# A new order for the opening of a fused layer norm, state-space scan and gated unit: roots by logarithm and exponential, four groups open, tiles turned in pairs

## The chip, the cores and the metric

The kernel runs on one core of one Trainium2 chip. Its time is device microseconds from the start to the end of one execution; runs of the kernel before gave 182.41, 182.43 and 182.47 us, median 182.43. A core has TensorE (PE: matrix products and transposes, which write to the eight banks of PSUM), VectorE (DVE), ScalarE (ACT: functions from loadable tables), GpSimd (POOL) and SyncE (SP, which here issues nearly all DMA transfers). Each engine takes its instructions strictly in its own order; they wait for each other by semaphores.

## The reference

The input is `x` of 2048 tokens by 448 features in bfloat16. Cut to what matters:

```python
xn = (x - mean(x)) / sqrt(var(x) + 1e-5)          # per token
# A: a diagonal complex scan over the tokens
Lam_bar = exp(exp(log_dt) * Lam)                  # 448 complex numbers
Bu = xn @ B_bar.T                                 # complex, 448 wide
h[t] = Lam_bar * h[t - 1] + Bu[t]
s = 2 * real(h @ C.T) + xn * Dskip
# B: a gated unit, 448 -> 1792 -> 448
d = (sigmoid(xn @ w_gate) * (xn @ w_up)) @ w_down
out = x + s * silu(d)
```

## The kernel before

The 2048 tokens are cut into four chunks of 512, a chunk into four blocks of 128 tokens. For a chunk, `xn` is made with tokens on the partitions and then turned, so that `xnT` has features on the partitions: four tiles `kt` of 128 rows that cover the 448 features. The 1792 columns of the gated unit are 14 groups `ft` of 128. A group needs two sums of 128 x 512 in PSUM, `g_ps` (gate) and `u_ps` (up), one bank each. 448 is three times 128 and 64 more, so a sum takes three products over 128 rows (`gu_wholes`) and one over 64 rows (`gu_halves`); the gate's 64 rows lie in partitions 0 to 63 of `wt` and the up's in 64 to 127, and the two run side by side in the two halves of the array. From the group `ft` 4 on, all products are cut into halves of 64 rows, the upper and the lower half run side by side (`beside_each`, line 507 in the profile), and a POOL instruction passes on that one half has ended before the other half adds to the same sum (a "word"). The state-space part makes `Bu` in units -1 to -4 (`bu_unit`), which stand among the groups; it turns `Bu` by a table of sines and cosines (`cosT`, `spm`) so that a real scan on VectorE does the complex one.

The order of the work is written by hand: `keep_order` ties every instruction to the one before it on its engine, in the order in which the Python code emits them. What this study is about is the opening, up to the first group that runs in halves (groups 4 and 5).

The steps of the opening, in the kernel before:

- DMA. ACT issues three short rows (`log_dt`, `Lambda_im`, `Lambda_re`, L141). SP issues the four token blocks of chunk 0 (one, one, and two in one transfer), the weights of groups 0 to 3 (`load_w(sync, 0, 512)`), those of groups 4 to 9, then the next chunk, and so on.
- TensorE. 31 products of an identity matrix with itself (`warm`, L195) whose result nobody reads; the three rows turned into columns (`turn_twice`, L200 to L202, into `tp_v`); the first two token blocks turned (`ln_turn`, four 128 x 128 transposes each, L282, into `tp_x`), a few warm products between; then groups 0 to 2 for the first 256 tokens, gates first, then ups; blocks 2 and 3 turned; and the rest of groups 0 to 3.
- Statistics. DVE takes mean and variance (`ln_stats`, L211 and L212) of blocks 0, 1 and 3; ACT takes those of block 2 (`ln_sum`, `ln_mean`, `ln_square`). The inverse root is a power of -0.5 on POOL (`ln_pow`, L241) behind an addition of epsilon. DVE normalises (`ln_norm`, L268) and copies the turned blocks from PSUM to `xnT` (`ln_out`, L285). `tp_x` is two tiles, one bank each; block 0 uses one and block 1 the other, and blocks 2 and 3 use them again.
- Constants. `emit_vecs` and `emit_angles` make the step angle and the decay; `emit_whole` (ACT, L417), `emit_frac` and `emit_abs` (DVE, L422 and L428) reduce the angles; `emit_sin` and `emit_cos` (ACT, L433 and L436) fill the second half of the tables, `emit_neg` (DVE, L445) negates, `emit_mirror` (POOL, L448 and L450) fills the first half by symmetry. The fractions and their absolute values have two buffers each.
- Evacuation. Groups 0 to 3 leave PSUM by a tanh on ACT (L713) and a copy on DVE (`up_copy`, L992). The sums of groups 4 and 5 are given the banks that the first of these free.
- ACT loads a table of functions three times: for the exponential (L923), for sine and tanh (L951), and for the sigmoid (L746).

The PSUM pool has eight buffers under one tag, so a ninth tile waits until the one whose place it takes has been read.

## Time and profile before

| | |
|---|---|
| median of three runs | 182.43 us |
| profiled execution, its own time | 182.76 us |
| its span, first to last instruction | 181.0 us |
| TensorE busy | 176.5 us, 98% |
| VectorE busy | 163.2 us, 90% |
| ScalarE busy | 114.2 us, 63% |
| GpSimd busy | 24.9 us, 14% |
| first product of groups 0 to 3 | 6.86 us |
| first product of groups 4 and 5 | 14.06 us |

How to read it: a timeline row has the start in us from the start of the span, the time it took, engine, source line, operation, tile written from tiles read, shapes, and how many were merged; a bracket names the idle time of the engine before it and what ended it. `128*128 128x256` is a product with 128 rows and 128 columns of weights over 256 moving columns. The time of a single product includes its way through the array (0.31 us for 128 columns before 6.6 us), so a row of several is read by the spacing of their starts. ACTq and SPq are rows of a sequencer that issues a transfer.

### The profile page before, as it was taken

The page shows a single profiled execution, that of the slowest core. Times are in us where ns is not written, and L with a number is a line of the kernel's source. Part 1 is how long each engine was busy: PE and PEld are TensorE (multiplying, and loading weights), DVE is VectorE, ACT ScalarE, POOL GpSimd, SP SyncE. Part 2 cuts the span into 40 slices and gives each one's busy share as a digit, 9 for nine tenths or more (in the row PEclk, how much of TensorE's full clock was granted, in tenths as well). Part 3 has the DMA queues.
Part 4 walks back from the last instruction along what each step waited for, and adds up shares of the span by engine and source line. Part 5 has one row for each costly group of instructions (what it writes and reads, how often), then busy time and mean ns, then how long its engine had stood idle before and what let it go on. Part 6 is the DMA issues. An engine that isn't in the chain of part 4 may idle for free.

```text
span 181.0 us, 4338 instructions
## 1 busy us (share of the span) xinstructions
PE 176.5 (98%) x1644; PEld 89.1 (49%) x1644; DVE 163.2 (90%) x332; ACT 114.2 (63%) x234; POOL 24.9 (14%) x59
## 2 busy tenths in 40 slices
PE   7999999999999999999999999999999999999993
PEld 7874444444544444544544444544554444545552
DVE  4799989999999869999999999599999999499993
ACT  3999678979577887988277767047137677144100
POOL 4786626513000000003000000000000000000000
PEclk9999999999999999999999999999999999999999
DMA  5899999993442104011610020020010100011012
GB/s 158 262 283 144 261 166 166 352 220 76 86 83 59 32 0 126 10 53 51 91 30 0 4 48 10 4 97 4 4 29 2 33 0 2 4 51 51 0 32 74
DMA packets 26347, 14.26 MB, mean 79 GB/s; under 512 B 16083, under 2 KB 26070, under 8 KB 26326
## 3 DMA queue, kind: packets, MB, share of 16 engines
q1 hardware_dynamic: 26320, 13.98, 34.5%
q8 instruction: 13, 0.21, 0.5%
q14 instruction: 8, 0.07, 0.1%
q10 hardware_dynamic: 6, 0.00, 0.0%
HBM read 7.69 MB, written 1.84 MB: 53 GB/s over the span
## 4 chain that ended last, share of the span: by engine, by line
PE 97%; DVE 1%; POOL 0%; issue 0%; POOLq 0%; DVEq 0%
PE g_ps L507 25%; PE u_ps L507 19%; PE d_ps L507 18%; PE bu L507 12%; PE y_ps L507 11%; PE d_ps L1106 6%; PE warm_ps L195 2%; PE g_ps L707 2%; PE u_ps L707 1%; PE tp_x L282 1%; PE g_ps L700 1%; DVE sg L854 0%; DVE o_l L860 0%; POOL ident L136 0%; POOL ident L135 0%
## 5 line engine op out<-in xcount | busy, mean ns | idle before, releaser
L507 PE MATMUL u_ps<-xnT,wu 64*128 64x512 bf16 x312 | 61.4, 376 | 0.0
L507 PE MATMUL g_ps<-xnT,wg 64*128 64x512 bf16 x312 | 53.4, 376 | 0.0
L746 ACT ACTIVATE sig<-g_ps 128x512 bf16<-128x512 f32 x52 | 29.2, 597 | 29.2 <-PE g_ps L507 28.6
L507 PE MATMUL bu<-xnT,bT 64*128 64x512 bf16 x168 | 37.4, 376 | 0.0
L507 PE MATMUL d_ps<-wd,hF 64*128 64x448 bf16 x336 | 32.3, 349 | 0.0
L507 PEld LDWEIGHTS <-wu 64*128 64x128 bf16 x312 | 22.4, 94 | 18.5
L746 ACT CAST ub<-u_ps 128x512 bf16<-128x512 f32 x52 | 29.3, 606 | 0.5 <-DVE hF L717 0.3
L507 PEld LDWEIGHTS <-wg 64*128 64x128 bf16 x312 | 18.9, 94 | 18.1 <-issue 0.2
L507 PEld LDWEIGHTS <-hF 64*128 64x128 bf16 x336 | 16.4, 94 | 15.6
L604 DVE TENSOR_TENSOR_SCAN wv<-r_col,st,ta 128x512 bf16<-128x512 f32 x18 | 22.7, 1276 | 0.2
L507 PE MATMUL y_ps<-ct,h 64*128 64x448 bf16 (+2 forms) x203 | 22.1, 343 | 0.0
L743 DVE TENSOR_TENSOR hF<-sig,ub 128x512 bf16<-128x512 bf16 x52 | 20.9, 413 | 0.4 <-ACT ub L746 0.3
L507 PEld LDWEIGHTS <-bT 64*128 64x128 bf16 x168 | 15.8, 94 | 10.0
L507 PE MATMUL g_ps<-xnT,wt 64*128 64x512 bf16 x52 | 19.6, 376 | 0.0
L507 PE MATMUL u_ps<-xnT,wt 64*128 64x512 bf16 x52 | 19.6, 376 | 0.0
L507 PEld LDWEIGHTS <-h 64*128 64x128 bf16 (+1 forms) x203 | 11.6, 95 | 9.9
L770 ACT ACTIVATE sigd<-d_ps 128x448 bf16<-128x448 f32 x12 | 6.6, 553 | 14.7 <-PE d_ps L507 14.7
L585 ACT CAST bus<-bu 128x512 bf16<-128x512 f32 x24 | 14.3, 597 | 2.2 <-PE bu L507 2.2
L241 POOL TENSOR_TENSOR rsd<-ve,mhalf 128x1 f32<-128x1 f32 (+2 forms) x8 | 6.9, 862 | 44.7 <-PE bu L507 43.9
L507 PEld LDWEIGHTS <-wt 64*128 64x128 bf16 x104 | 9.8, 94 | 6.2
L825 DVE TENSOR_TENSOR o_t<-y_ps,xn 128x448 bf16<-128x448 f32 x12 | 6.9, 618 | 4.8 <-PE y_ps L507 4.8
L1106 PE MATMUL d_ps<-wd,hF 128*128 128x448 bf16 x56 | 10.9, 353 | 0.0
(149 smaller groups left out, 238.5 us busy)
## 6 DMA issues: line engine op xcount, KB each, us to landing
wd<-in_B_w_down_dram SPq DMA_DIRECT2D x1, 1568.0 KB, 7.7
x<-in_A_x_dram SPq DMA_DIRECT2D x3, 448.0 KB, 6.4
out_dram<-o_t SPq DMA_DIRECT2D x6, 224.0 KB, 2.1
wg<-in_B_w_gate_dram SPq DMA_DIRECT2D x2, 256.0 KB, 3.1
wu<-in_B_w_up_dram SPq DMA_DIRECT2D x2, 256.0 KB, 3.6
bsw<-bus SPq DMA_DIRECT2D x4, 128.0 KB, 3.3
wsw<-wv SPq DMA_DIRECT2D x8, 64.0 KB, 1.9
c_re<-in_A_C_re_dram SPq DMA_DIRECT2D x1, 392.0 KB
```

The lines of the kernel that those rows point to most:

```text
L195: pe.matmul(warm_ps[:], lhsT=ident[:], rhs=ident[:], start=True, stop=True)
L241: pool.tensor_tensor(out=rsd[:, t:t + n, :], in0=ve[:, t:t + n, :], in1=mhalf[:, 0:n, :], op=ALU.pow)
L282: pe.transpose(tps[j % 2][:, kt, :], xb[:, j, K_ROWS[kt]:K_ROWS[kt] + P], ident[:])
L507: m = pe.matmul(self.t[:, n0:n1], lhsT=lhsT, rhs=rhs, start=self.done == 1, stop=self.done == self.n)
L585: empty = [lambda cc=cc: act.copy(out=bus[:, cc, :], in_=pst[cc][:]) for cc in range(2)]
L604: dve.tensor_tensor_scan(out=T["wv"][:, cc, :], data0=rb, data1=T["ta"][:, cc, :], initial=(0.0 if c == 0 else st[pt][:, cc, :]), op0=mul, ...
L707: pe.matmul(t[:, n0:n1], lhsT=wm[:, k, f0:f1], rhs=xnT[c][:, kt, n0:n1], start=(first and k == 0), stop=(not first and k == 2))
L743: dve.tensor_tensor(out=h[:], in0=sig[:], in1=ub[:], op=ALU.mult)
L746: u.empty = [lambda: act.activation(sig[:], gt[:], ACT.Sigmoid), lambda: act.copy(out=ub[:], in_=ut[:])]
L770: act.activation(sigd[:], ds[j][:], ACT.Sigmoid)
L825: dve.tensor_tensor(out=two_runs(o[:, i, :], HD, HD), in0=two_runs(ys[c, j + 2 * i][:], HD, HD), in1=xn_runs(c, j + 2 * i), op=ALU.add)
L1106: pe.matmul(ds[j][:], lhsT=hF[c, ft][:, j * P:(j + 1) * P], rhs=wd[:, ft, :], start=ft == 0, stop=ft == FT - 1)
```

## The change

It touches the opening only.

- The inverse roots of chunk 0 are made by ACT, as the exponential of -0.5 times the logarithm (`ln_inv`), and no longer by POOL. ACT's first table is one that holds both functions; it is loaded by an explicit instruction.
- The three rows are turned after 7 warm products, and 19 follow; ACT copies them out of PSUM, and the angles, steps and denominators follow at once on POOL.
- All eight sums of groups 0 to 3 are given their banks before the first product. `tp_x` is still two banks, but a bank holds two turned blocks: blocks 0 and 1 are turned into the first, blocks 2 and 3 into the second.
- All four groups' gates for the first 256 tokens come first, then the transposes of blocks 2 and 3, then all four ups, then all products over 64 rows (first and second 256 tokens), then the remaining products over 128 rows. So TensorE changes between 128-row and 64-row products three times.
- Fractions and absolute values come after the copies of blocks 2 and 3; the index products on ACT come after the fourth root.
- The mirrors go to groups 5 (two of them), 8 and 11; before, two were in the opening and two at group 5.
- For groups 4 to 9, the 64-row weights are loaded before the up weights.

```diff
-    def load_w(eng, f0, f1):
+    def load_w(eng, f0, f1, tails_first=False):
...
-        eng.dma_start(out=wu[:, 0:2, f0:f1], in_=rows(B_w_up, 0, 256))
-        eng.dma_start(out=wu[:, 2, f0:f1], in_=rows(B_w_up, 320, 448))
-        eng.dma_start(out=wt[0:64, f0:f1], in_=rows(B_w_gate, 128, 192))
-        eng.dma_start(out=wt[64:128, f0:f1], in_=rows(B_w_up, 256, 320))
+        up = ((wu[:, 0:2, f0:f1], rows(B_w_up, 0, 256)), (wu[:, 2, f0:f1], rows(B_w_up, 320, 448)))
+        tails = ((wt[0:64, f0:f1], rows(B_w_gate, 128, 192)), (wt[64:128, f0:f1], rows(B_w_up, 256, 320)))
+        for o, i in (tails + up if tails_first else up + tails):
+            eng.dma_start(out=o, in_=i)
...
-    load_w(sync, 512, 1280)
+    load_w(sync, 512, 1280, True)
...
-    def ln_pow_of(t, n, var, scale):
-        pool.tensor_scalar(out=ve[:, t:t + n, :], in0=var, scalar1=scale, scalar2=EPS, op0=ALU.mult, op1=ALU.add)
-        ln_pow(t, n)
+    lnv = w.tile([P, TPC, 1], FP32, name="lnv")
+
+    def ln_inv(t, var, scale=1.0):
+        act.activation(lnv[:, t, :], var, ACT.Ln, bias=epsb[:], scale=scale)
+        act.activation(rsd[:, t, :], lnv[:, t, :], ACT.Exp, scale=-0.5)
...
-            pe.transpose(tps[j % 2][:, kt, :], xb[:, j, K_ROWS[kt]:K_ROWS[kt] + P], ident[:])
+            pe.transpose(tps[j // 2][:, j % 2, kt, :], xb[:, j, K_ROWS[kt]:K_ROWS[kt] + P], ident[:])
 
     def ln_out(j):
-        dve.tensor_copy(out=xnT[0][:, :, j * P:(j + 1) * P], in_=tps[j % 2][:])
+        dve.tensor_copy(out=xnT[0][:, :, j * P:(j + 1) * P], in_=tps[j // 2][:, j % 2, :, :])
...
-        dve.tensor_copy(out=vec[:], in_=tp_v[:, :, 0:3])
+        act.copy(out=vec[:], in_=tp_v[:, :, 0:3])
...
-    act.activation(dummy[:], hpi[:], ACT.Exp)
-    warm(31)
-
-    ln_stats(0)
-    ln_pow_of(0, 1, mv[:, 0:1, 1:2], 1.0)
-    ln_stats(1)
-    ln_root(1, 1)
+    act.add_instruction(mybir.InstLoadActFuncSet(name=nc.get_next_instruction_name(), act_func_set_id=LN_AND_EXP,
+                                                 ins=[], outs=[]))
+    warm(7)
+    turn_twice(tp_v, rows, 3)
+    emit_vecs()
+    emit_angles()
+    emit_steps()
+    emit_den()
+    tps = [ps.tile([P, 2, KT, P], BF16, name="tp_x", tag="bank", bufs=8) for _ in range(2)]
+    gus = [(bank("g_ps"), bank("u_ps")) for _ in range(4)]
+    warm(19)
+
+    for j in range(2):
+        ln_stats(j)
+        ln_inv(j, mv[:, j, 1:2])
     ln_sum(2)
-    turn_twice(tp_v, rows, 3)
-    tps = [ps.tile([P, KT, P], BF16, name="tp_x", tag="bank", bufs=8) for _ in range(2)]
     ln_norm(0, 0)
     ln_turn(0, 0)
-    emit_vecs()
-    emit_angles()
-    warm(2)
+    ln_norm(0, 1)
+    ln_turn(0, 1)
+    warm(4)
+    ln_out(0)
+    ln_out(1)
     ln_mean(2, 1)
     ln_square(2)
-    ln_pow_of(2, 1, sums[:, 2:3, 1:2], 1.0 / D)
-    ln_norm(0, 1)
-    ln_turn(0, 1)
-    warm(5)
-    ln_out(0)
-    ln_out(1)
+    ln_inv(2, sums[:, 2, 1:2], 1.0 / D)
     ln_stats(3)
+    ln_inv(3, mv[:, 3, 1:2])
+    act.activation(K["r"][:], K["arg"][:], ACT.Exp)
     for pt in (0, 1, 3, 2):
         emit_whole(pt)
-    act.activation(K["r"][:], K["arg"][:], ACT.Exp)
-
     act.activation(dummy[:], hpi[:], ACT.Silu)
-    ln_pow_of(3, 1, mv[:, 3:4, 1:2], 1.0)
-
-    gus = [(bank("g_ps"), bank("u_ps")) for _ in range(3)]
-    for ft in range(3):
+
+    for ft in range(4):
         gu_wholes(0, ft, *gus[ft], True, 0, HC, (0,))
-    for ft in range(3):
-        gu_wholes(0, ft, *gus[ft], True, 0, HC, (1,))
-    ln_norm(0, 2)
-    ln_turn(0, 2)
-    emit_frac(0)
-    ln_norm(0, 3)
-    ln_turn(0, 3)
-    emit_abs(0)
+    for j in (2, 3):
+        ln_norm(0, j)
+        ln_turn(0, j)
     for j in (2, 3):
         ln_out(j)
-    emit_frac(1)
-    emit_abs(1)
-    emit_frac(3)
-    emit_abs(3)
-    emit_frac(2)
-    emit_abs(2)
-    for ft in range(3):
-        gu_halves(0, ft, *gus[ft], False, 0, HC)
-    gus.append((bank("g_ps"), bank("u_ps")))
-    gu_wholes(0, 3, *gus[3], True, 0, HC)
-    gu_halves(0, 3, *gus[3], False, 0, HC)
+    for pt in (0, 1, 3, 2):
+        emit_frac(pt)
+        emit_abs(pt)
     for ft in range(4):
-        gu_halves(0, ft, *gus[ft], True, HC, TC)
+        gu_wholes(0, ft, *gus[ft], True, 0, HC, (1,))
+    for n0 in (0, HC):
+        for ft in range(4):
+            gu_halves(0, ft, *gus[ft], n0 > 0, n0, n0 + HC)
     for ft in range(4):
         gu_wholes(0, ft, *gus[ft], False, HC, TC)
-    emit_steps()
-    emit_den()
...
-    for pt in (0, 1):
-        emit_mirror(pt)
-    for pt in (3, 2):
-        at(0, 5, 0.0, lambda pt=pt: emit_mirror(pt))
+    for pt, ft in ((0, 5), (1, 5), (2, 8), (3, 11)):
+        at(0, ft, 0.0, lambda pt=pt: emit_mirror(pt))
```

## The prediction

> **What bounds the kernel now.** I read the page's busy shares and its chain that ended last, then the timeline of TensorE (PE) until it no longer waits, then VectorE (DVE), ScalarE (ACT) and POOL beside it.
>
> ```profile
> PE 176.5 (98%) x1644; PEld 89.1 (49%) x1644; DVE 163.2 (90%) x332; ACT 114.2 (63%) x234; POOL 24.9 (14%) x59
> PE 97%; DVE 1%; POOL 0%; issue 0%; POOLq 0%; DVEq 0%
> ```
>
> TensorE is busy for 98% of the span and 97% of the last chain. In the windows view, 14.06 to 160.00 has TensorE busy for all 145.94 us. So the end stands at a fixed distance behind 14.06, where the steady groups (L507) begin: 181.0 - 14.06 = 166.9 us. The change is in front of that point, so the question is when the first L507 starts.
>
> ```profile
> 1.35 3.49 PE L195 MATMUL warm_ps<-ident 128*128 128x128 bf16 x31 [1.35 <-POOL ident L136]
> 4.77 0.23 PE L200 MATMUL tp_v<-ident,rows 3*128 3x3 bf16 x3
> 5.10 0.61 PE L282 MATMUL tp_x<-ident,xn 128*128 128x128 bf16 x4
> 5.74 0.61 PE L282 MATMUL tp_x<-ident,xn 128*128 128x128 bf16 x4
> 6.14 0.74 PE L195 MATMUL warm_ps<-ident 128*128 128x128 bf16 x5
> 6.86 1.14 PE L707 MATMUL g_ps<-xnT,wg 128*128 128x256 bf16 x9
> 8.82 0.73 PE L282 MATMUL tp_x<-ident,xn 128*128 128x128 bf16 x8
> 11.33 0.50 PE L707 MATMUL g_ps<-xnT,wg 128*128 128x256 bf16 x3
> 14.06 0.82 PE L507 MATMUL g_ps<-xnT,wg 64*128 64x512 bf16 x6
> ```
>
> Until 6.86 TensorE mostly does warm-up products (L195); from 6.86 to 14.06 it does real work without a hole. The spacing tells the clock: 31 warm products in 3.49 us are 0.107 us apart ((3.49 - 0.31) / 30), and so still at 6.14 to 6.57; from 6.86 on 256 columns take 0.109 each, half the price per column. The full clock came between 6.57 and 6.86. (The PEclk row shows 9 throughout and does not tell this.)
>
> What releases 6.86 is the normalisation of the first two token blocks:
>
> ```profile
> 4.14 0.18 DVE L212 BATCH_NORM_AGGREGATE mv<-stats 128x2 f32<-128x6 f32 x1
> 5.29 0.39 DVE L268 TENSOR_SCALAR xn<-x,mv,rsd 128x448 bf16<-128x448 bf16 x1
> 5.75 0.42 DVE L285 COPY xnT<-tp_x 128x512 bf16<-128x512 bf16 x1
> 6.39 0.42 DVE L285 COPY xnT<-tp_x 128x512 bf16<-128x512 bf16 x1 [0.21 <-PE tp_x L282]
> ```
>
> Second variance at 4.32, normalised block at 5.68, turned from 5.74, copied by 6.81, first product at 6.86. The first copy ran while the second block was still being normalised and turned.
>
> ScalarE and DVE release the PSUM banks that the first L507 group writes:
>
> ```profile
> 8.20 1.28 ACT L951 ACT_TABLE_LOAD   x1
> 9.60 0.40 ACT L433 ACTIVATE spm<-frac 128x256 bf16<-128x256 f32 x1
> 9.90 0.49 ACT L436 ACTIVATE cosT<-afrac,hpi 128x256 bf16<-128x256 f32 x1
> 12.02 1.17 ACT L713 ACTIVATE tanh<-g_ps 128x512 f32<-128x512 f32 x2
> ```
>
> The first tanh ends near 12.6, the first u copy (DVE L992, from 12.55) near 13.2: 0.9 us or more ahead of 14.06.
>
> **The change, part by part.**
>
> *Vectors first.* The row transposes move ahead of 19 warm products, behind 7. They need three row loads that ACT issues at 0.72, 1.27 and 1.51, as before; the trace's semaphore record has the last one landing at 3.10 (bounds: the x blocks' 2.0 us from issue to landing gives 3.5; the second row, 2.69). So TensorE does 7 warm products until 2.1, idles about 1 us, does the five row transposes from 3.14 (0.33, from 4.77 to 5.10 in the trace), then 19 x 0.107 = 2.03: until 5.50. The first token transposes stand behind them. That is the change's main price: with 31 warm products ahead, this queue was empty at 4.6.
>
> *Inverse roots.* POOL's two instructions (0.19 + 0.6, ready at 4.55 and 5.15) go; ACT gets a logarithm and an exponential for each block. No row shows a logarithm. Small activations take 0.18 to 0.21; a pointer as bias adds 0.09 (sine 0.40, cosine with hpi 0.49); so 0.28 + 0.04 + 0.19 = 0.51 a pair. Bounds: 0.42 without the pointer's share, and 1.0 if a logarithm cost as much as the 448-wide square (0.67, L228). ACT now does the vector copy (about 0.2, DVE's was 0.17) and dt first: 3.58 to 4.04. The first root is ready at 4.46, the second at 4.88 (behind its variance at 4.32). Normalised blocks at 4.89 and 5.31: earlier than before, but both before TensorE is free at 5.50. This gain is covered by the warm products; even the 1.0 bound moves the second block only to about 5.8, against the 5.93 at which its transposes start.
>
> *Pairs.* Both blocks are turned in 8 x 0.107: last start 6.25, end 6.56. They now share one bank and one tile, and the built order has the first copy wait for the last transpose of the second block. So the two copies stand one behind the other: 6.59 + 0.77 (two copies at 9.25 took that) = 7.36, and the first L707 at 7.4 instead of 6.86. One copy more on the path is worth 0.35 of that.
>
> *TensorE from there.* The same 48 products of 256 columns (5.23) and 8 pairs of 64-row products (8 x 0.11 = 0.88). A change of row mode costs 0.10: at 10.68 and 11.33 the step is 0.205 instead of 0.109. After: 12 gate products to 8.71; third block turned to 8.93; the fourth waits for its root. DVE: copies to 7.36, statistics and aggregate as from 6.73 (0.83) to 8.12; ACT 0.05 + 0.51 = 8.68; normalised at 9.1; turned from 9.15 to 9.43, a hole of 0.2. Then 12 up products to 10.74 (the copies that free the last bank end at about 10.3), change, 8 pairs, change, 24 products, change: 10.74 + 0.10 + 0.88 + 0.10 + 2.62 + 0.10 = 14.54. That is 7.14 against 7.20: two changes saved, 0.2, and nearly as much lost to the hole.
>
> *ACT and DVE up to the banks.* The four index products (L417, 1.69) now stand behind the fourth root: 8.69 to 10.36; table load 1.28 to 11.65; dummy; first sine 11.76 instead of 9.60. Three pairs of sine and cosine at ACT's own pace (0.30 + 0.40, and 0.10 more for the third) 2.2: tanh at 13.96 to 14.54, so the second L507 matmul can start at 14.59. DVE's fractions share two buffers with the sines; the last one's absolute value waits for the second cosine and ends near 13.75, the negation follows, the first u copy (0.64) ends near 14.6. All three chains arrive between 14.54 and 14.65. I take 14.6.
>
> *Edits at nothing.* Steps and denominators earlier on POOL: it idles there. Mirrors later, with groups 5, 8 and 11: two at group 5 took 16.01 to 18.42 before with no hole in TensorE, and the ones at 8 and 11 go where POOL waits (3.08 us before L377, 0.40 before L390); if the last held the words with which POOL relays one half's end to the other, it would cost up to its 1.0. Tails first: same bytes on SP's queue in the same time; before, all of that load was in by 13.93, and what comes last now is needed at about 15.5. Behind 14.6 DVE is 1.3 us late against before, and so are the norms of the second chunk and four DMA transposes on SP, by some 0.8 (landed 31.1, needed near 33); the 0.90 of DVE at 27.41, waiting for skip, takes up the rest.
>
> **Sum.** 14.6 - 14.06 = +0.54: span 181.54. The profiled execution took 182.76 with its span of 181.0; the median of the runs, 182.43, is 0.33 below it. I add the 0.54 to the median: 182.97.
>
> **Rivals.**
>
> *The queue is not in the way (not slower).* If the last row lands by about 2.55, or the full clock comes by about 5, TensorE is free when the second block is normalised (5.31): eight transposes end near 6.1, copies 6.9, first product 6.94, steady groups at 14.1. Time 182.45, no change that a measurement of this kernel can tell (about 0.2%, 0.36 us). It decides from a row landing 0.5 us sooner than the record says. This is also the floor: the path from the variance at 4.32 through root, norm, transposes and two copies leaves nothing to gain before 6.94, and saved mode changes are 0.2 at most. Faster by more than 0.36 needs something that I don't see in the rows.
>
> *A late clock (slower still).* Before, TensorE worked from 1.35 almost without a hole, and the full clock came some 5.4 us later. Now it idles from 2.1 to 3.1. If the count starts anew at 3.14, the clock comes near 8.6, and from 7.4 to 8.6 products run at half pace: 0.6 lost, steady groups at 15.2, 183.57. Against it: between 3.4 and 6.8, the stretch before the clock rose, TensorE is busier in the changed kernel than before. The Trainium skill, page "TensorE: Matmul & The Clock Gate", Part 1, says that the gate judges activity in a free-running window of about 3.4 us; by that rule the clock would come at the same 6.8 if the window stands as before, and later only if the hole falls into the window that counts, and no run here shows where it stands in other executions.
>
> **How the numbers follow.** The forecast (queue, two copies, three chains at 14.6) 0.56; the not slower rival 0.24; the late clock 0.13; something that I haven't seen and that makes it faster 0.07. The likeliest case's own range is 182.7 to 183.2: a row landing 0.2 us sooner or later moves everything one for one. For 8 in 10 the range reaches to the second case's time and nearly the third's: 182.4 to 183.5. Slower by more than 0.36 (over 182.79): the third, and 0.49 of the first, 0.62; within: 0.07 of the first and 0.24, 0.31; faster 0.07.
>
> **What the profile after would show.** Right: a hole in TensorE from about 2.1 to 3.1; row transposes near 3.1; first token transposes at 5.5 straight behind warm products, though xn was done near 4.9; both copies back to back after the second block's transposes; first L707 near 7.4; table load near 10.4; first tanh near 14; first L507 near 14.6, and no hole after. Wrong: row transposes before 2.7; 128-column products closer than 0.107 before 6; L707 spaced 0.21; a hole in TensorE behind the steady start.

## The result and the profile after

The changed kernel takes 184.54 us (median of 184.20, 184.51, 184.57 and 184.62); the kernel before, run beside it, 182.45 us. The ratio is 1.0111, with a 95% interval of 1.0094 to 1.0129. It is slower, as forecast, but by 2.1 us where 0.54 was forecast, and beyond the range, which ended at 183.5. The profiled execution took 184.62 us with a span of 182.8; that of before 182.76 with 181.0. So the two profiles show 1.86 of the 2.1 us. Beside each set of the experiments below the kernel before was run again, 17 to 35 times, with medians of 182.75 to 182.78; against these the 184.54 is 1.8 more.

Busy times and the chain that ended last, from the page of the changed kernel:

```profile
PE 175.9 (96%) x1636; PEld 149.9 (82%) x1636; DVE 164.3 (90%) x331; ACT 115.4 (63%) x242; POOL 22.8 (12%) x52
PE 87%; DVE 6%; ACT 2%; issue 1%; DMA 1%; POOL 1%; ACTq 0%; DVEq 0%; POOLq 0%
```

TensorE has hardly less to do (175.9 against 176.5 us), but it is no longer the whole of the last chain: 87% instead of 97%. DVE, ACT, a DMA and POOL have come in. The timeline of TensorE up to the steady groups (L507):

```profile
1.35 0.93 PE L198 MATMUL warm_ps<-ident 128*128 128x128 bf16 x7 [1.35 <-POOL ident L137]
3.50 0.21 PE L203 MATMUL tp_v<-ident,rows 3*128 3x3 bf16 x3 [1.23 <-DMA rows<-in_A_Lambda_re_dram]
3.81 2.21 PE L198 MATMUL warm_ps<-ident 128*128 128x128 bf16 x19
5.81 1.06 PE L282 MATMUL tp_x<-ident,xn 128*128 128x128 bf16 x8
7.72 1.47 PE L707 MATMUL g_ps<-xnT,wg 128*128 128x256 bf16 x12 [0.42 <-DVE xnT L285]
9.02 0.84 PE L282 MATMUL tp_x<-ident,xn 128*128 128x128 bf16 x8
9.70 1.52 PE L707 MATMUL u_ps<-xnT,wu 128*128 128x256 bf16 x12
14.98 0.82 PE L507 MATMUL g_ps<-xnT,wg 64*128 64x512 bf16 x6
```

The hole for the rows is there (1.23 us), 19 warm products stand behind it, the token transposes start straight behind those at 5.81, and TensorE waits 0.42 for both copies. The first real product comes at 7.72, 0.86 later than before; the steady groups at 14.98, 0.92 later. DVE beside it:

```profile
4.78 0.90 DVE L268 TENSOR_SCALAR xn<-x,mv,rsd 128x448 bf16<-128x448 bf16 x2
6.91 0.76 DVE L285 COPY xnT<-tp_x 128x512 bf16<-128x512 bf16 x2 [1.24 <-PE tp_x L282]
17.31 1.89 DVE L717 SCALAR_TENSOR_TENSOR hF<-tanh,ub 128x512 bf16<-128x512 f32 x2
```

The second block is normalised at 5.68, 0.13 before TensorE is free; the copies come one behind the other. The last row matters below: these two products took 1.28 us at 15.42 before.

The steady groups do not run through. The view of TensorE's waits between 14 and 30 us has one row:

```profile
PE g_ps L507 <- POOLq L509: 0.6, 1, 0.6
```

L509 is the word by which POOL passes on that one half has ended. Between 22.34 and 23.28 no product starts; a pair of halves otherwise starts every 0.216 us, so the hole is 0.73. The chain that ended last, between 14 and 24 us (start, time, what):

```profile
17.39 1.81 DVE hF L717 x2
...
20.72 0.18 DVE ve L241
...
20.97 1.10 POOL rsd L244
22.07 1.14 issue
23.21 0.03 POOLq L509
23.23 0.05 issue
23.28 0.39 PE g_ps L507
```

What that "issue" is, POOL's timeline tells:

```profile
20.97 1.10 POOL L244 TENSOR_TENSOR rsd<-ve,mhalf 128x2 f32<-128x2 f32 x1 [0.49 <-DVE ve L241]
23.25 1.21 POOL L244 TENSOR_TENSOR rsd<-ve,mhalf 128x2 f32<-128x2 f32 x1 [1.18 <-DVE ve L241]
```

POOL's second root for the next chunk waits 1.18 us for DVE's `ve` (variance plus epsilon), until 23.25. The word stands behind it in POOL's queue, and 0.03 us after that wait ends, TensorE goes on.

Reckoned by when products start: the last one comes at 179.32 instead of 177.57, +1.76 before rounding. The opening is +0.92, the hole +0.73; 0.11 is spread over the rest and not traced.

### The profile page after: what moved, and what is told of

It reads as the page before. It is cut to its first block, busy times and chain, and to the rows that moved or that the text cites. A ratio compares the mean times of both kernels' runs of the same rounds, so it can differ in the third digit from the quotient of the medians.

```text
span 182.8 us, 4323 instructions
## 1 busy us (share of the span) xinstructions
PE 175.9 (96%) x1636; PEld 149.9 (82%) x1636; DVE 164.3 (90%) x331; ACT 115.4 (63%) x242; POOL 22.8 (12%) x52
## 3 DMA queue, kind: packets, MB, share of 16 engines
q1 hardware_dynamic: 26320, 13.98, 31.3%
## 4 chain that ended last, share of the span: by engine, by line
PE 87%; DVE 6%; ACT 2%; issue 1%; DMA 1%; POOL 1%; ACTq 0%; DVEq 0%; POOLq 0%
PE g_ps L507 20%; PE u_ps L507 19%; PE d_ps L507 17%; PE y_ps L507 11%; PE bu L507 11%; PE d_ps L1093 6%; DVE ub L981 1%; PE warm_ps L198 1%; DMA rows<-in_A_Lambda_re_dram 1%; DVE hF L717 1%; DVE stats L214 1%; ACT whole L417 1%; ACT L954 1%; POOL rsd L244 1%; DVE frac L422 0%
## 5 line engine op out<-in xcount | busy, mean ns | idle before, releaser
L507 PE MATMUL u_ps<-xnT,wu 64*128 64x512 bf16 x312 | 58.1, 376 | 0.0
L507 PE MATMUL g_ps<-xnT,wg 64*128 64x512 bf16 x312 | 56.7, 376 | 0.6 <-POOLq L509 0.6
L507 PE MATMUL bu<-xnT,bT 64*128 64x512 bf16 x168 | 37.0, 376 | 0.0
L507 PEld LDWEIGHTS <-wg 64*128 64x128 bf16 x312 | 28.4, 94 | 6.0 <-POOLq L509 1.1
L507 PEld LDWEIGHTS <-wu 64*128 64x128 bf16 x312 | 28.7, 94 | 5.2
L507 PE MATMUL d_ps<-wd,hF 64*128 64x448 bf16 x336 | 32.5, 349 | 0.0
L507 PEld LDWEIGHTS <-hF 64*128 64x128 bf16 x336 | 31.3, 94 | 0.6
L507 PE MATMUL y_ps<-ct,h 64*128 64x448 bf16 (+2 forms) x203 | 22.4, 343 | 0.0
L507 PEld LDWEIGHTS <-h 64*128 64x128 bf16 (+1 forms) x203 | 19.1, 95 | 2.4
L507 PE MATMUL g_ps<-xnT,wt 64*128 64x512 bf16 x52 | 19.6, 376 | 0.0
L507 PE MATMUL u_ps<-xnT,wt 64*128 64x512 bf16 x52 | 19.6, 376 | 0.0
L507 PEld LDWEIGHTS <-bT 64*128 64x128 bf16 x168 | 15.7, 94 | 2.9
L507 PEld LDWEIGHTS <-wt 64*128 64x128 bf16 x104 | 9.8, 94 | 1.7
L244 POOL TENSOR_TENSOR rsd<-ve,mhalf 128x2 f32<-128x2 f32 (+1 forms) x4 | 5.2, 1302 | 45.4 <-PE bu L507 43.7
```

Source lines behind the costliest of these rows:

```text
L244: pool.tensor_tensor(out=rsd[:, t:t + n, :], in0=ve[:, t:t + n, :], in1=mhalf[:, 0:n, :], op=ALU.pow)
L507: m = pe.matmul(self.t[:, n0:n1], lhsT=lhsT, rhs=rhs, start=self.done == 1, stop=self.done == self.n)
```

## The experiments

Fourteen kernels were run. This table has, for the profiled execution of each: when the last row landed, the first product of groups 0 to 3, from when the trace's record has the full clock, the first steady group, the hole behind it, and the last product, and then the median of all executions and that of the kernel before beside it. All in us.

| kernel | row in | first L707 | full clock | first L507 | hole | last product | median | before |
|---|---|---|---|---|---|---|---|---|
| before | 3.10 | 6.86 | 6.81 | 14.06 | 0 | 177.57 | | 182.45 |
| changed | 3.36 | 7.72 | 7.56 | 14.98 | 0.73 | 179.32 | 184.54 | 182.45 |
| e1_root_later | 3.23 | 7.58 | 8.55 | 14.95 | 0 | 178.45 | 183.69 | 182.78 |
| e2_fewer_warm | 3.26 | 7.08 | 9.50 | 15.15 | 0 | 178.95 | 183.99 | 182.78 |
| e3_own_banks | 3.29 | 7.31 | 7.94 | 14.57 | 0.73 | 178.92 | 184.12 | 182.78 |
| e4_rows_late | 3.40 | 7.15 | 4.73 | 14.41 | 0.73 | 178.75 | 183.95 | 182.78 |
| c1_root_own | 3.30 | 7.03 | 8.90 | 14.86 | 0 | 178.36 | 183.83 | 182.76 |
| c2_filled | 3.35 | 6.60 | 5.12 | 13.81 | 0 | 177.36 | 182.70 | 182.76 |
| b2_hole | 3.26 | 6.80 | 8.49 | 14.69 | 0 | 178.19 | 183.42 | 182.76 |
| b1_act_roots | 3.31 | 6.58 | 7.28 | 13.98 | 0 | 177.49 | 182.67 | 182.76 |
| c3_filled_pairs | 3.24 | 7.02 | 6.49 | 14.28 | 0 | 177.83 | 183.03 | 182.76 |
| c4_filled_root_back | 3.29 | 6.67 | 4.96 | 13.74 | 0.74 | 178.10 | 183.38 | 182.76 |
| e5_mirrors_later | 3.15 | 7.50 | 7.78 | 14.76 | 0.73 | 179.11 | 184.21 | 182.76 |
| d1_best | 3.27 | 6.61 | 6.27 | 13.88 | 0.45 | 177.85 | 182.65 | 182.76 |
| f1_mirrors_behind | 3.33 | 7.68 | 7.20 | 14.94 | 0 | 178.55 | 183.99 | 182.75 |
| d2_before_best | 3.39 | 6.38 | 5.14 | 13.94 | 0 | 177.45 | 182.62 | 182.75 |

The last product is the first L507 plus the hole plus 163.5 to 163.8 in every row, so these two columns and the hole are what the end hangs on. The experiments ran in four sets, each on another chip (e1 to e4; c1, c2, b1 and b2; c3, c4, e5 and d1; f1 and d2). The kernel before has a median of 182.75 to 182.78 in them and 182.45 beside the changed kernel, and its single executions range from 182.40 to 184.74; a step of less than 0.3 between two sets is not read.

### The root one group later

```diff
-    at(0, 7, 1.0, lambda: second_chunk(2))
-    at(0, 7, 0.0, lambda: sync.dma_start(out=wd[:], ...))
+    at(0, 8, 1.0, lambda: second_chunk(2))
+    at(0, 8, 0.0, lambda: sync.dma_start(out=wd[:], ...))
...
```

> The changed kernel with the second inverse root of the second chunk (L244 on POOL, with the norms and turns behind it, the wd load and both C loads) emitted one group later, at (0,8) instead of (0,7). Theory A (the second half of the loss): in the changed kernel POOL waits 1.18 us for DVE's ve at 22.07 to 23.25, and the word that lets TensorE go from one half to the other stands behind that wait, so TensorE has a hole of 0.73 us until 23.28. With the root one group later the word comes first: no hole over 0.3 us between 15 and 27 us, and a time lower by about 0.7 us, near 183.8 beside 184.5 for the changed kernel. The opening stays: first L507 at 14.98. Theory B (the hole is TensorE waiting for PSUM banks that DVE frees late, whatever POOL's order): the hole stays at about 22.3 to 23.3 and the time stays near 184.5.

Measured: 183.69 us, ratio to before 1.0045 (1.0014 to 1.0076). The hole is gone; TensorE is busy without a break, where the changed kernel loses 0.63. The windows from 14.50 to 30.00 us (length, then busy time of PE, its weight loads, DVE, ACT and POOL, clock, DMA share, GB/s), first the changed kernel, then this one:

```profile
14.50:30.00 15.50, 14.87 (x137) 9.96 (x137) 15.26 (x36) 12.52 (x26) 8.57 (x15) 1.00 0.91 176
```

```profile
14.50:30.00 15.50, 15.50 (x145) 7.05 (x145) 15.26 (x37) 12.95 (x28) 10.41 (x16) 1.00 0.93 174
```

The opening stayed (14.95), and DVE's `ve` for the second root still starts only at 22.66; now the words pass ahead of that wait. Theory B falls. The edit moves three loads and the norms and turns along with the root; the kernel with the mirrors behind the roots, further down, leaves all of these in place and has no hole either, so they are not what makes it.

### Fewer warm products in the way

```diff
-    warm(19)
+    warm(14)
...
-    warm(4)
+    warm(9)
```

> The changed kernel with 14 warm products instead of 19 between the row transposes and the token transposes, and 9 instead of 4 behind the token transposes. Theory A (the queue of warm products is on the path): token transposes of block 0 start near 5.3, when its normalised tile is ready, those of block 1 near 5.7 when the second norm ends (5.68 in the changed kernel); first L707 near 7.25 instead of 7.72, steady groups near 14.5 instead of 14.98, time lower by 0.4 to 0.5 us, if the hole at 22 to 23 us keeps its length. Theory B (the norms or the late full clock set it, not the queue): first L707 stays near 7.7, or it comes at 7.25 and runs 0.4 us at half pace up to 7.56, so that the steady groups start no sooner than 14.8; time within 0.15 us of the changed kernel.

Measured: 183.99 us (1.0024 to 1.0086 of before). Both theories were half right. The queue was in the way: the transposes start at 5.17 and the first product at 7.08. But it ran slowly:

```profile
5.17 1.06 PE L282 MATMUL tp_x<-ident,xn 128*128 128x128 bf16 x8
7.08 2.63 PE L707 MATMUL g_ps<-xnT,wg 128*128 128x256 bf16 x12
9.55 0.61 PE L282 MATMUL tp_x<-ident,xn 128*128 128x128 bf16 x8
15.15 0.82 PE L507 MATMUL g_ps<-xnT,wg 64*128 64x512 bf16 x6
```

From 7.08 to 9.55 are 12 products, 0.206 us each; in the changed kernel 12 took 1.30, from 7.72 to 9.02. The full clock came only at 9.50, and the steady groups came later than in the changed kernel, at 15.15. That also hid the hole: the late clock held TensorE and not DVE, whose hF began at 16.90 instead of 17.31 and took 1.48 instead of 1.89. So POOL's second root ended its wait for `ve` at 22.42 instead of 23.25, and TensorE came to the word only at 22.71.

### Tiles of their own

```diff
-            pe.transpose(tps[j // 2][:, j % 2, kt, :], ...)
+            pe.transpose(turned(j)[:, kt, :], ...)   # block 0: first bank; 1 and 3, 2: halves of the second
```

> The changed kernel with the token transposes put into tiles of their own again, so that the copy of block 0 waits for block 0's transposes alone; nothing else is moved. Theory A (the pairing puts two copies one behind the other on the path): first copy near 6.5, beside block 1's transposes, second copy from 6.9 to 7.35, first L707 near 7.35 instead of 7.72, steady groups near 14.6, time lower by 0.3 to 0.4 us. Theory B (DVE is late for both copies for another reason): the first copy still starts at 6.9 and the first L707 at 7.7; no change of time over 0.15 us.

Measured: 184.12 us. First product 7.31, steady groups 14.57, both 0.41 sooner than in the changed kernel, as theory A has it (0.07 of it is the rows, turned at 3.43 here and at 3.50 there). The first copy starts at 6.41 beside block 1's transposes:

```profile
6.41 0.85 DVE L289 COPY xnT<-tp_x 128x512 bf16<-128x512 bf16 x2 [0.89 <-PE tp_x L286]
```

The hole is 0.73 again, though all is 0.4 sooner.

### The rows late again

```diff
-    warm(7)
-    turn_twice(tp_v, rows, 3)
-    emit_vecs()
-    emit_angles()
-    emit_steps()
-    emit_den()
...
-    warm(19)
+    warm(31)
...
+    turn_twice(tp_v, rows, 3)
+    emit_vecs()
+    emit_angles()
+    emit_steps()
+    emit_den()
     ln_norm(0, 0)
```

> The changed kernel with vectors first undone: 31 warm products without a break, then the row transposes, then vectors, angles, steps and denominators, then norms and token transposes. Theory A (it is the wait for the rows with 19 products behind it that is on the path): no hole in TensorE between 1.35 and 5; row transposes at about 4.8, token transposes of block 0 at about 5.3, of block 1 at about 5.7, first L707 near 7.25; the full clock near 6.8 as in the kernel before instead of 7.56; steady groups near 14.5; time lower by about 0.45 us. It should come out like the run with fewer warm products. Theory B (the clock counts from the last hole and that is what costs): more is won than with fewer warm products, 0.6 us or more.

Measured: 183.95 us. First product 7.15, as expected; the full clock at 4.73, sooner than I expected; steady groups at 14.41 (0.57 sooner), where they wait for a bank: TensorE's last up product had started at 14.08, and 0.33 passed, where the kernel before has 0.20. The bank comes from DVE's first u copy, which ended at 14.35, 0.05 before; one of the fractions ahead of it had waited 0.41 for ACT's first sine. So beyond this the chain of sines on ACT and of fractions and u copy on DVE holds the start. The hole is 0.73 again. Of the median, 0.6 was won against 184.54, as much as with fewer warm products, as theory A has it; the ten executions spread from 183.44 to 184.64.

### Is it the hole in front of the rows? Two kernels that differ in warm products only

The first has the root one group later, tiles of their own, and 7, 14 and 9 warm products; the second has 18, 12 and 6:

```diff
-    warm(7)
+    warm(18)
...
-    warm(14)
+    warm(12)
...
-    warm(9)
+    warm(6)
```

> The changed kernel with three things undone together: the second inverse root one group later, token transposes into tiles of their own, and 14 and 9 warm products in place of 19 and 4. The hole in TensorE before the rows land (2.3 to 3.4 us) stays. In the runs so far the full clock lasted exactly 174.08 or 177.49 us (51 or 52 times 3.413) and came at 4.7 to 9.5 us from the start, so theory A is: the clock is judged in free-running windows of 3.413 us, and a window that holds the hole does not count. Then the first L707 comes near 6.9, the clock at any time from about 6.9 to 10.3, and what is worked before it goes at half pace: executions spread over more than 0.5 us, lowest near 182.5, median 182.9 to 183.4. Theory B (queue, paired copies and POOL's held word are all there is): L707 near 6.9 and steady groups near 14.1 in every execution, time as the kernel before within 0.2 us, and a spread like that of the kernel before.

> As the kernel just named, but TensorE is kept busy while the rows come: 18, 12 and 6 warm products in place of 7, 14 and 9 (one more... 36 instead of 30 in all). Theory A (free-running windows of the clock): with no hole from 1.35 on, the full clock comes between about 4.8 and 8.2 us, so nearly all real work runs at full clock: median 0.3 us or more below the kernel with the hole, and a narrower spread. Theory B (the hole is harmless): the same median within 0.15 us. Both expect the first L707 near 6.8 to 6.9 and no hole behind the steady start; with theory A the time is that of the kernel before within 0.3 us.

Measured: 183.83 us (183.61 to 184.09) with the hole, 182.70 (182.56 to 183.24) without. The first products, with the hole, then filled:

```profile
7.03 2.40 PE L711 MATMUL g_ps<-xnT,wg 128*128 128x256 bf16 x12
```

```profile
6.60 1.48 PE L711 MATMUL g_ps<-xnT,wg 128*128 128x256 bf16 x12 [0.23 <-DMA wg<-in_B_w_gate_dram]
```

The difference is 1.13 us. With the hole 12 products take 2.40, for the full clock comes at 8.90; filled, 1.48, with the clock at 5.12. Not all of the 1.13 is the clock: nine warm products at half clock behind the transposes hold the first kernel until 7.03, six the second until 6.37, and then it waits for weights until 6.60. With the hole, the median is above the 182.9 to 183.4 of theory A, and the lowest time, 183.61, is not the 182.5 that it gave; with four executions, that stays open.

### The hole alone, in the kernel before

```diff
-    warm(31)
+    warm(7)
+    turn_twice(tp_v, rows, 3)
+    warm(10)
...
-    turn_twice(tp_v, rows, 3)
```

> The kernel before, with only the row transposes moved ahead: 7 warm products, row transposes when the rows land, 10 warm products, and then all as before. TensorE idles from 2.3 to about 3.3 us, and is free again at about 4.8 as before; all other engines are as before. Theory A (free-running windows of the clock): first L707 near 6.9 as before, but the full clock comes at 6.9 to 10.3 us instead of 4.8 to 8.2, the 256-column products before it stand 0.21 us apart, and the time rises by half of what is worked before the clock: median 0.4 to 0.9 us above the kernel before, the highest executions 1.3 to 1.7 above its lowest, the lowest equal to its lowest. Theory B (a hole of 1 us costs the clock nothing): within 0.15 us of the kernel before.

Measured: 183.42 us (183.02 to 184.30) against 182.76, ratio 1.0051 (1.0033 to 1.0068). This is the cleanest of the runs: the other engines are no later than they were (DVE's vector copy, and what hangs on it on ACT and POOL, is 0.3 sooner), the first product comes at 6.80 (before: 6.86), and yet the steady groups come 0.63 later.

```profile
3.39 0.22 PE L200 MATMUL tp_v<-ident,rows 3*128 3x3 bf16 x3 [1.12 <-DMA rows<-in_A_Lambda_re_dram]
6.80 1.95 PE L707 MATMUL g_ps<-xnT,wg 128*128 128x256 bf16 x9
14.69 0.82 PE L507 MATMUL g_ps<-xnT,wg 64*128 64x512 bf16 x6
```

Nine products that took 1.14 take 1.95, 0.81 more; the clock came at 8.49. A hole of 1.1 us that ends 3.4 us before there is real work costs 0.66 us of the median, and as no engine is later in the profile up to the first product, it is the clock that costs it. The lowest execution, 183.02, is not as low as before's lowest, against theory A's detail.

### Pairs, without the hole

c2 with the pairs kept; against c2:

```diff
-            pe.transpose(turned(j)[:, kt, :], ...)
+            pe.transpose(tps[j // 2][:, j % 2, kt, :], ...)
```

> The changed kernel with the second inverse root one group later and TensorE kept busy while the rows come (18, 12 and 6 warm products instead of 7, 19 and 4); the token transposes stay in pairs. It differs from the filled run before it only in the pairs. Theory A (the pair puts both copies one behind the other in front of the first product): copies start near 6.1 to 6.3 and end near 7.0, first L707 near 7.05 against 6.60, steady groups 0.2 to 0.45 us later, median 182.9 to 183.1. Theory B (something else is as late, so the pair costs nothing): median 182.7 within 0.1.

Measured: 183.03 us (182.81 to 183.21) against 182.70; first product 7.02 against 6.60, steady groups 14.28 against 13.81.

```profile
6.21 0.76 DVE L285 COPY xnT<-tp_x 128x512 bf16<-128x512 bf16 x2 [0.71 <-PE tp_x L282]
```

Both copies stand in front of the first product. The pair costs 0.42 us at the first product and 0.33 us of the median; the two ran in different sets, in both of which the kernel before has 182.76, and 0.33 is little over what is read between sets.

### The root at its place, with an early opening

Against c2:

```diff
-    at(0, 8, 1.0, lambda: second_chunk(2))
+    at(0, 7, 1.0, lambda: second_chunk(2))
...
```

> The filled run with tiles of their own, but with the second inverse root at its place in the changed kernel, (0,7). Theory A (a word held behind POOL's wait for DVE's ve; DVE's chain is later against TensorE in the changed order whatever the opening does): the hole in TensorE near 21 to 22.5 us comes back with 0.4 to 0.9 us, and the median is 0.4 us or more above 182.7. Theory B (the held word matters only with the late opening of the changed kernel): no hole over 0.3 us, median 182.7 within 0.15.

Measured: 183.38 us (183.29 to 183.76), 0.68 above c2 of the set before. The waits of TensorE between 14 and 30 us:

```profile
PE g_ps L511 <- POOLq L513: 0.6, 1, 0.6
```

The hole is back with 0.74, though the steady groups start at 13.74, before those of the kernel before. DVE is no later here than in c2: its second `ve` starts at 21.77, there at 21.83. So it is the order of POOL's queue, and not the late opening, that makes the hole. In all five kernels with it, the hole ends 8.30 or 8.31 us behind the first L507 (for the changed kernel 23.28 - 14.98), whenever that is. Both ends of that stretch hang on DVE: in these five the first L507 starts 0.05 us behind the end of DVE's first u copy, for which it waits, and from there DVE goes on to hF, the statistics and `ve`.

### Why is DVE late? The mirrors

```diff
-    for pt, ft in ((0, 5), (1, 5), (2, 8), (3, 11)):
+    for pt, ft in ((0, 6), (1, 6), (2, 8), (3, 11)):
```

> The changed kernel with the first two mirrors at group 6 instead of group 5; nothing else. In the changed kernel they run on POOL from 16.91 to 19.68, beside DVE's two hF products (L717), which then take 1.89 instead of the 1.28 of the kernel before. Theory A (the mirrors beside it slow DVE): hF back to about 1.3, DVE's ve and with it POOL's second root 0.4 to 0.6 us sooner, the hole at 22.3 to 23.3 us shorter by as much, time lower by 0.3 to 0.6 us. Theory B (DVE is late through the fractions and u copies alone): hF stays near 1.9 or the hole keeps its 0.73, time within 0.15 us of 184.5.

Measured: 184.21 us, and nothing moved: POOL has nothing to wait for in front of the mirrors, so they ran from 16.69 instead of 16.91, and hF took 1.89. So this decides nothing between the theories. It is a near copy of the changed kernel, with a hole of 0.73 and ten executions from 183.44 to 184.42. The next edit puts them behind both roots:

```diff
-    for pt, ft in ((0, 5), (1, 5), (2, 8), (3, 11)):
+    for pt, ft in ((0, 8), (1, 8), (2, 8), (3, 11)):
```

> The changed kernel with the first two mirrors emitted at group 8, behind POOL's two inverse roots of the second chunk, so that POOL cannot start them before 22 us (at group 6 they still ran at 16.69). Theory A (the mirrors beside DVE's two hF products make DVE late, and through its ve POOL's second root and the word behind it): hF takes 1.3 instead of 1.89 us, ve comes about 0.6 us sooner, the hole of 0.73 us in TensorE near 22 to 23 us shrinks to 0.1 to 0.2 us, time lower by 0.5 to 0.6 us, near 183.7 to 183.9. Theory B (the fractions and the u copies alone make DVE late): hF is still 1.89 or the hole stays above 0.5 us, time 184.1 to 184.6.

Measured: 183.99 us (183.76 to 184.14). DVE's products:

```profile
17.07 1.29 DVE L717 SCALAR_TENSOR_TENSOR hF<-tanh,ub 128x512 bf16<-128x512 f32 x2
```

```profile
22.42 1.21 POOL L244 TENSOR_TENSOR rsd<-ve,mhalf 128x2 f32<-128x2 f32 x1 [0.88 <-DVE ve L241]
```

hF takes 1.29, the second `ve` starts 0.83 sooner, the second root at 22.42 instead of 23.25, and TensorE has no hole. Theory A holds, for the profile: the mirrors cost DVE 0.6, and that 0.6 and 0.2 of a negation (0.22 instead of 0.41) made the hole. The steady groups still start at 14.94 and the last product comes 0.77 sooner. The median fell by 0.55 against the changed kernel's, but only by 0.22 against the near copy just above, so the medians alone do not show it. The Trainium skill, page "SBUF — State Buffer", section "SBUF: two separate sides", says that DVE and GpSimd share a pair of ports as an exclusive lock, which a DVE operation with two inputs in SBUF takes against a GpSimd operation that reads SBUF. hF reads `tanh` and `ub` from there and the mirrors read `cosT` and `spm`; 1.89 beside them and 1.29 without them agree. In these runs the one that starts first keeps its time: in c1, as in the kernel before, hF began ahead of the first mirror (16.61 and 16.80), and there hF took 1.29 and that mirror 1.35 instead of 0.40.

### Is there a version that beats both?

The kernel before with the first two roots on ACT, ahead of the vectors (in full: `ln_inv` and the table as in the change, DVE's vector copy behind the second norm, 26 warm products):

```diff
-    ln_pow_of(0, 1, mv[:, 0:1, 1:2], 1.0)
+    ln_inv(0, mv[:, 0, 1:2])
     ln_stats(1)
-    ln_root(1, 1)
+    ln_inv(1, mv[:, 1, 1:2])
```

> The kernel before, with only the inverse roots of the first two blocks changed: logarithm and exponential on ScalarE right behind each variance, the vector copy on DVE behind the second norm, and 26 warm products instead of 31 so that the token transposes find TensorE free. Theory A (roots on ScalarE are worth their time if nothing is queued in front of them): roots ready near 4.1 and 4.8, normalised blocks near 4.6 and 5.3 instead of 4.98 and 5.68, first L707 near 6.4 instead of 6.86, steady groups near 13.6 to 13.8, time 0.2 to 0.5 us below the kernel before unless the u weights (in at 7.5 to 7.8) hold TensorE. Theory B (ScalarE's roots are no sooner than POOL's, or the weights or the clock take the gain back): first L707 at 6.8 or later, or a wait of TensorE at the u products, time within 0.15 us of the kernel before.

Measured: 182.67 us against 182.76, ratio 1.0022 (0.9992 to 1.0052). The first product comes at 6.58, 0.28 sooner, but at half clock until 7.28, and the steady groups at 13.98. Theory B, by way of the clock.

Two more, with warm products on a tile that DVE sets first, so that they start at 1.04 instead of 1.35: one on c2 (with the roots ahead of the vectors, and the k slice that lands last multiplied last), one on the kernel just above.

```diff
+    hot = w.tile([P, P], BF16, name="hot")
+    dve.memset(hot[:], 1.0)
...
-            pe.matmul(warm_ps[:], lhsT=ident[:], rhs=ident[:], start=True, stop=True)
+            pe.matmul(warm_ps[:], lhsT=hot[:], rhs=hot[:], start=True, stop=True)
```

> The filled run with tiles of their own and the root one group later, and three things more: warm products on a tile that DVE sets first (so they can start near 0.95 instead of 1.35, 22 of them ahead of the row transposes), the two roots on ScalarE ahead of the vector copy, and in the opening groups the k slice that lands last is multiplied last. Theory A (the opening is bound by the chain from the second variance at 4.32 through root, norm, turn and copy, and by the weights landing at 6.5): first L707 near 6.3, steady groups near 13.6, full clock between 4.4 and 7.8, median 182.4 to 182.6, 0.2 us below the kernel before. Theory B (the third and fourth block, whose roots follow on ScalarE, or the banks take it back): first L707 near 6.3 but steady groups at 13.8 or later, median 182.7 to 182.8.

> The kernel before with the first two inverse roots on ScalarE ahead of the vector copy (as in the earlier run), and warm products on a tile that DVE sets first, so that TensorE can start near 1.04 instead of 1.35; 29 of them ahead of the row transposes. Theory A (the opening is bound by TensorE and the clock): first L707 near 6.5, full clock between about 4.4 and 7.8 us, steady groups at 13.6 to 13.9, median 182.4 to 182.6, 0.1 to 0.3 us below the kernel before. Theory B (something behind the opening holds the end, as the steady groups at 13.81 and 13.88 of two runs gave no more than 0.1 us): median 182.65 to 182.8.

Measured: 182.65 us (ratio 0.9994, 0.9968 to 1.0020) and 182.62 (1.0004, 0.9987 to 1.0021): no change that can be measured. In the second, the first product comes at 6.38 at full clock, then the u weights hold it:

```profile
7.68 1.31 PE L718 MATMUL u_ps<-xnT,wu 128*128 128x256 bf16 x9 [0.17 <-DMA wu<-in_B_w_up_dram]
8.83 0.61 PE L293 MATMUL tp_x<-ident,xn 128*128 128x128 bf16 x8
```

and the third and fourth block are turned at 8.83, where they were turned before (8.82). In the first, steady groups begin at 13.88, and 0.45 is lost at 21.02, where TensorE waits for a transposed `B` that DMA brought at 21.64 in that execution. The medians fall between the two theories, and in both profiles a load holds part of what the opening gives. No version was found that beats the kernel before by more than the measurements can tell.

## Why the prediction was wrong

The sign was right and the size wrong by 1.6 us. By its steps:

*Vectors first.* The price is there, and was put too low. Row transposes at 3.50, not 3.14; warm products until 5.81, not 5.50. The landing at 3.10 came from one execution, and in all 16 traces the last row lands from 3.10 to 3.40: that one is the lowest. To that came 0.14 from landing to the first transpose where I had put 0.04. The sentence "a row landing 0.2 us sooner or later moves everything one for one" was right, and its middle value was not.

*Inverse roots.* 0.28 and 0.20 a pair, as forecast. They came 0.3 late (4.74 and 5.22), since the vector copy on ACT waited for the rows and block 1's `x` landed at 3.79 instead of 3.23; the second block was normalised at 5.68, and its transposes started at 6.24. Covered by the warm products, as forecast, with 0.56 to spare.

*Pairs.* Right: copies at 6.91 behind each other, first product 7.72, of which the pair makes 0.34 (e3, without its earlier rows); alone it costs 0.33 of the median (c3 against c2).

*TensorE from there.* 7.26 instead of 7.14. The hole at the fourth block is there (the second four transposes at 9.47 behind the first at 9.02); the three changes of row mode are as forecast. At the end TensorE waits 0.12 for the banks, the "three chains" of the forecast; the last of them is DVE's first u copy, which ended at 14.93. Steady groups 14.98 instead of 14.6: of the 0.38, 0.31 is the late rows.

*Edits at nothing.* This is the step that failed, and "a hole in TensorE behind the steady start" was one of the signs of being wrong that the prediction named. DVE and POOL before, and POOL's first mirror after:

```profile
15.42 1.28 DVE L717 SCALAR_TENSOR_TENSOR hF<-tanh,ub 128x512 bf16<-128x512 f32 x2
16.01 0.96 POOL L448 COPY cosT<-cosT 128x255 bf16<-128x255 bf16 x1 [1.36 <-PE u_ps L507]
20.79 1.21 POOL L241 TENSOR_TENSOR rsd<-ve,mhalf 128x2 f32<-128x2 f32 x1 [0.52 <-DVE ve L238]
```

```profile
16.91 0.40 POOL L448 COPY cosT<-cosT 128x255 bf16<-128x255 bf16 x1 [9.26 <-ACT tanh L713]
```

"The mirrors ... at group 5 took 16.01 to 18.42 before with no hole in TensorE" was true, but before, hF had begun at 15.42, ahead of them, and it was the first mirror that took 0.96 instead of 0.40; now the mirrors begin at 16.91, ahead of hF at 17.31, and hF takes 0.61 more. "Behind 14.6 DVE is 1.3 us late ... and so are the norms of the second chunk ... the 0.90 of DVE at 27.41, waiting for skip, takes up the rest": DVE was 2.5 us late (statistics at 19.13 instead of 16.62), and I followed that to the norms and the DMAs but not to POOL, whose root waits for DVE and whose queue holds TensorE's words behind it. I had named such a held word for the last mirror and not for the root. The root had waited before as well, until 20.79, and TensorE came to the words behind it at 21.62: there were 0.83 us to spare. In the changed kernel TensorE would have come 0.93 later, at 22.55, and the wait ended 2.46 later. The cost is 0.73 us in the profile; 0.68 of the median where it was put back alone (c4 against c2).

*The late clock.* As a rival it had a chance of 0.13, and the clock does come late, though not in the profiled execution: there the clock came at 7.56, just ahead of the first product at 7.72. In eight kernels with the hole in front of the rows it came between 7.20 and 9.50, in eight without it between 4.73 and 7.28. b2 shows its price alone, 0.66 of the median where the first product comes at 6.80. In the changed kernel the first product is itself late, so that less of the real work runs at half clock (none in this execution; 0.46 in e1, whose 12 products took 1.93), and a late clock delays TensorE and not DVE, so that the held word can come in time, as in e2. So how much of the changed kernel's 2.1 us is clock was not measured; it varies from one execution to the next.

*The queue is not in the way* fell: e2 and e4 bring the first product forward by 0.6.

Undone one after the other, the medians go from 184.54 (184.21 for its near copy e5) to 183.69 with the root one group later, to 183.03 with TensorE kept busy in front of the rows and fewer products in the way, to 182.70 with tiles of their own; the kernel before has 182.76. These three are the loss. What is left of the change in c2, four groups open, three changes of row mode, roots on ACT, mirrors late and tails first, neither gains nor loses.

## What to carry to other kernels

A queue that passes on signals for others must not hold an instruction that waits for a third engine: when an edit makes an engine late, follow what it releases through every queue, not only through the arrays it writes. Waiting for a transfer a little earlier on TensorE can cost time even where only warm products stand around the wait, for the clock comes later (0.66 us in b2); move such a wait behind work that fills it. A landing time from one execution is one draw: take the range from several, and look whether the one at hand is at its edge.

## What the runs showed of the hardware

The full clock lasted 174.08 us in twelve traces and 177.49 in four. The two differ by 3.413 us and are 51 and 52 times that, and in all traces the full clock ended 2.3 to 5.3 us after the last product. Where TensorE worked without a hole from its first product on, the full clock came 3.4 to 5.9 us after that; where it had a hole until about 3.4, it came 3.7 to 6.1 us after the hole's end. That is what windows of 3.41 us would give that run on without regard to where a kernel starts, if a window with a hole of about 1 us in it does not count. It is a reading that fits the 16 traces; no run set where the windows stand. The Trainium skill, page "TensorE: Matmul & The Clock Gate", Part 1, gives 3413 ns and a free-running window; the traces agree. The rival in the prediction took from it that the clock would stay at 6.8 "if the window stands as before"; in the eight traces with the hole it came at 7.20 or later.

The busy time of the weight loads says little of the pace. In the five kernels with a hole behind POOL's word, PEld is 82 or 83% of the span (149.9 us in the changed kernel), and also in f1, which has no such hole; in eight others 48 to 52%, in c2 and c3 71%, while products keep their pace of 0.216 us a pair and a load of the steady groups still shows 94 ns. How the two halves stand against each other may set it; that was not tried, and no time was seen to hang on it.
